# Reading matmul operands backwards and weaving the two words of each weight, in four forms

## The chip, the cores and the metric

The kernel runs on one core of a Trainium2 chip. The metric is the device time of one execution in microseconds; three runs of the kernel before gave 804.3 to 804.74 us with a median of 804.55 us. The core has a matrix engine (TensorE; in the views PE for its matmuls and PEld for its weight loads), a vector engine (VectorE, DVE), a scalar engine (ScalarE, ACT), GpSimd (POOL), and DMA queues that SyncE (SP) issues here.

## The reference

Everything is in 32-bit floating point. A retention layer (attention with a decay in place of a softmax) is followed by two multilayer perceptrons (MLPs) over 2304 tokens of 512 values:

```python
scores = scale * np.matmul(q, k.transpose(0, 1, 3, 2))
ret = scores * Dmat[None, :, :, :]                 # decay by distance, causal
x = np.matmul(ret, v)                              # (4, 8, 576, 64) -> (2304, 512)
...
h = np.maximum(x @ w_in, 0.0)                      # first MLP, 512 -> 2048
x = h * h @ w_out                                  # 2048 -> 512
...
h = x @ w_in2                                      # second MLP, 512 -> 2048
g = h * np.clip(h + 3.0, 0.0, 6.0) / 6.0
out = g @ w_out2                                   # 2048 -> 512
```

## The kernel before, in words

A product of two 32-bit numbers is made from three matmuls in a shorter format (float32r). Each operand is split into a high word (a cast) and a low word (the operand minus its high word), and a product is high times high, plus low times high, plus high times low. Every tile that a matmul reads therefore has a dimension of 2: index 0 is the high word, index 1 the low one.

**First MLP.** Tokens go in five blocks of 512, 384, 512, 384 and 512 (BLOCKS); a block's tokens are the columns that move through TensorE. The hidden dimension goes in 16 tiles of 128, numbered f. For each f there are two weight tiles, w_f_0 (for w_in) and w_f_1 (for w_out), each with 128 partitions, two words and 512 values. They are loaded and split once, in the first block, and stay for all five. The split is cast_w on ScalarE (the high word, L167) and low_w on GpSimd or VectorE (the low word, L174). h_part (L623) makes one hidden tile h with 12 matmuls: three products of words by four slices of 128 input values. ScalarE and VectorE turn h into the two words of its squared positive part, the tile g. a_part (L660) adds that tile's share to the four accumulators acc with 12 matmuls. The main loop emits h_part for the next f ahead of a_part for this one, so TensorE's order is h of f+1, acc of f, h of f+2, acc of f+1, and so on. In between stand the small matmuls of the retention layer for later tokens (L408 to L496) and, on the other engines, the preparation of the second MLP's weights.

**Second MLP.** It runs in three superblocks s of 768 tokens, each as seven products of half size in place of eight (Strassen's scheme in Winograd's form). In each superblock first come 336 matmuls of 384 columns (L1183, out to the PSUM banks z, weights from the tiles ring, columns from the tiles xop), and then 504 matmuls of 256 columns (L1238, weights from the tiles spl, columns from ring).

Where tiles lie in SBUF is set by the order of allocation and by three tiles that nothing uses: `align` (80 values) moves what lies on the right side, and `shift0` and `shift1` move the tiles spl by 64 bytes:

```python
    SHIFT, FIRST_SHIFT = 64 // 4, 192 // 4
    p1a.tile([P, SHIFT], F32, tag="shift0", name="shift0")
```

With these, the operands of L623, L660 and L1183 all begin at the same place modulo 512 bytes, and the weights of L1238 begin 64 bytes (modulo 128) away from its columns.

The program's order is written out by hand (manual_schedule); each engine runs its instructions in that order.

Of the kernel before, what the change touches and what calls it, by code (L numbers as in the profile page):

```python
# [12 lines left out]
F32R = mybir.dt.float32r  # L13
# [73 lines left out]
def retention_moe_kernel(ctx: ExitStack, tc, qk, kv, w1, w2, cst, out):  # L87
# [30 lines left out]
    ctx.enter_context(tc.manual_schedule())  # L118


    raws = {}
    wts = {}
    narrowed = [0]
# [38 lines left out]
    def cast_w(ph, f, halves=(0, 1)):  # L162

        for i in halves:
            t = wts[ph, f, i]
            w = (wlo if f < NJ else whi).tile([P, 2, DM], F32R, tag=f"w{f}_{i}", name=f"w_{ph}_{f}_{i}")
            nc.scalar.activation(w[:, 0, :], t, AF.Copy)  # L167
            wts[ph, f, i] = w, t

# [441 lines left out]
    def h_part(ph, blk, f, between=lambda: None):  # L611
        nb = BLOCKS[blk][0]
        w = wts[ph, f, 0]
        x = xs[ph, blk]
        hp = ps_h.tile([P, 512], F32, tag="h", name=f"h_{ph}_{blk}_{f}")
        def order(last):
            return [(c, wi, xi) for wi, xi in ((0, 0), last[::-1], last) for c in range(NC)]

        parts = 2 if ph == blk == f == 0 else 1
        for i in range(parts):  # L620
            ts = slice(i * nb // parts, (i + 1) * nb // parts)
            for k, (c, wi, xi) in enumerate(order((1, 0) if blk == 0 and i == 0 else (0, 1))):
                nc.tensor.matmul(  # L623
                    hp[:, ts],
                    w[:, wi, c * P : (c + 1) * P],
                    x[:, xi, c, ts],
                    start=k == 0,
                    stop=k == 3 * NC - 1,
                )
        r = tmpp.tile([P, 512], F32, tag="tmp", name=f"r_{ph}_{blk}_{f}")  # L630
        r = r[:, :nb]
        nc.scalar.activation(r, hp[:, :nb], AF.Relu)  # L632
        between()
        nc.vector.tensor_tensor(r, r, hp[:, :nb], ALU.mult)  # L634
        g = gpool.tile([P, 2, 512], F32R, tag="g", name=f"g_{ph}_{blk}_{f}")
        nc.scalar.activation(g[:, 0, :nb], r, AF.Copy)  # L636
        gts[ph, blk, f] = g, r
# [7 lines left out]
    def a_part(ph, blk, f):  # L645
        nb = BLOCKS[blk][0]
        w = wts[ph, f, 1]
        g = gts.pop((ph, blk, f))
        if f == 0:
            two = [  # L650
                ps_acc.tile([P, 2, 512], F32, tag="acc", name=f"acc_{ph}_{blk}_{d}")
                for d in range(2)
            ]
            accs[ph, blk] = [two[d // 2][:, d % 2, :] for d in range(NC)]
        acc = accs[ph, blk]
        last = f == NF - 1

        def mm(d, wi, gi, first, stop):
            wt = w[:, wi, d * P : (d + 1) * P]
            nc.tensor.matmul(acc[d][:, :nb], wt, g[:, gi, :nb], start=first, stop=stop)  # L660

        if last:
            for d in range(NC):
                mm(d, 0, 0, False, False)
                mm(d, 1, 0, False, False)
                mm(d, 0, 1, False, True)
        else:
            for d in range(NC):
                mm(d, 0, 0, f == 0, False)
                mm(d, 1, 0, False, False)  # L670
            for d in range(NC):
                mm(d, 0, 1, False, False)
# [488 lines left out]
    for s in range(SUPERS):  # L1161
        t_a = now + NJ * 7 * t_in

        for m, (q, k) in enumerate((q, k) for q in ORDER for k in range(NJ)):
            free = t_a + (m - NSPL + 1 + 1.6 * ((s, q) == FINAL and k >= NSPL)) * t_out / NJ
            if m < NSPL:
                free = max(free, now + (k + 1) * 7 * t_in + 1.0)
            at(free + 0.1, a_cast, s, q, k)
            at(free + 0.7, a_low, s, q, k)
        for j in range(NJ):  # L1170
            e = j % 2
            bank = {q: z[k][:, :HALF] for q, k in H_BANK[e].items()}
            s1, u2 = held[2 * e][:, 0, :], held[2 * e][:, 1, :]
            u3 = held[1][:, e, :]
            c22, c21, c12 = s1, u3, u2
            for i, q in enumerate(ORDER):
                run(now)
                w = wring[s, 0, j, i // 2][:, i % 2]
                x = x_ops[q]
                for k, (u, wi, xi) in enumerate(  # L1180
                    [(u, wi, xi) for wi, xi in ((0, 0), (1, 0), (0, 1)) for u in range(2)]
                ):
                    nc.tensor.matmul(  # L1183
                        bank[q],
                        w[:, wi, u * P : (u + 1) * P],
                        x[:, u, xi, :],
                        start=k == 0 and q not in (2, 4, 3),
                        stop=k == 5,
                        skip_group_check=q in (2, 4, 3),
                    )  # L1190
                now += t_in
                if i % 2 or i == 6:
                    ring_done(now + 0.1)
                if q == 1:
                    at(now, act, s1, bank[1], AF.Copy)
                elif q == 6:
                    at(now, tt, u2, bank[6], s1, ALU.add)
                elif q == 7:
                    at(now, tt, u3, bank[7], u2, ALU.add)
                elif q == 5:  # L1200
                    at(now, tt, c22, bank[5], u3, ALU.add)
                    at(now + 0.8, relu3, 4, j, c22)
                    at(now + 1.3, gate, 4, j, c22)
                elif q == 2:
                    at(now, relu3, 1, j, bank[1])
                    at(now + 0.75, gate, 1, j, bank[1])
                elif q == 4:
                    at(now, tt, c21, bank[4], u2, ALU.add)
                    at(now + 0.8, relu3, 2, j, c21)
                    at(now + 1.3, gate, 2, j, c21)  # L1210
                else:
                    at(now, tt, c12, bank[3], u2, ALU.add)
                    at(now + 0.8, relu3, 7, j, c12)
                    at(now + 1.3, gate, 7, j, c12)
                    at(now + 2.0, pool_op, 5, 7, 4, ALU.add, j)
                    at(now + 2.1, pool_op, 7, 1, 7, ALU.subtract, j)
                    at(now + 2.2, pool_op, 6, 5, 1, ALU.subtract, j)
                    at(now + 2.3, pool_op, 3, 2, 6, ALU.subtract, j)
        if s + 1 < SUPERS:
            for u, st in enumerate(x_stages(s + 1)):  # L1220
                for k, part in enumerate(st):
                    at(now + 1.0 + 25.0 * u * (k > 0) + 3.0 * k + 4.0 * (k > 0), do, part)
        s1, u3, u2 = [h.rearrange("p a b -> p (a b)") for h in held]
        for i, q in enumerate(ORDER):
            work = [(k, (0, 1, 2)) for k in range(NJ)]
            if (s, q) == FINAL:

                work = [(k, (0, 1)) for k in range(LAG)]
                for k in range(NJ):
                    work += [(k, (2,))] + [(k + LAG, (0, 1))] * (k + LAG < NJ)  # L1230
            to = {2: (0, 0, None), 5: (1, 1, u3), 4: (1, 0, u2), 3: (0, 1, u2)}
            for k, parts in work:
                run(now)
                w, sp = wring[s, 1, q, k // 2], splits[s, q, k]
                for n in parts:
                    o = z[A_BANKS[q][n // 2]][:, HALFD * (n % 2) : HALFD * (n % 2 + 1)]
                    for m, (g, wi) in enumerate(((0, 0), (0, 1), (1, 0))):
                        nc.tensor.matmul(  # L1238
                            o,
                            sp[:, g, P * n : P * (n + 1)],  # L1240
                            w[:, k % 2, wi, :],
                            start=k == 0 and m == 0 and n % 2 == 0 and q not in (2, 4, 3),
                            stop=k == NJ - 1 and m == 2 and n > 0,
                            skip_group_check=q in (2, 4, 3),
                        )
                now += t_out / NJ / NTT * len(parts)
                if k % 2 and 2 in parts:
                    ring_done(now + 0.1)
                if q in to and k == NJ - 1:
                    pieces = [i for i in range(2) if PIECES[i][0] in parts]  # L1250
                    at(now, emit, now, s, q, *to[q], pieces)
            if q not in to:
                at(now, merge, q, *{1: (s1, None), 6: (u2, s1), 7: (u3, u2)}[q])
# [39 lines left out]
```

## Time and profile before

| what | before |
|---|---|
| device time, median of 3 runs | 804.55 us (804.3 to 804.74) |
| span of the profiled execution, first to last instruction | 802.6 us |
| TensorE matmuls busy, instructions | 796.4 us (99%), 6380 |
| TensorE weight loads busy, instructions | 741.0 us (92%), 6380 |
| VectorE, ScalarE, GpSimd busy | 591.9, 397.5, 167.7 us |
| TensorE's granted clock, mean | 1.000 |

The profiled execution has no device time of its own on record: its span is 802.6 us, and the median of the runs is 1.95 us more. A matmul's duration in the profile reaches from its start to a modelled end, and matmuls overlap, so the rate of a row of them is read from the distance of their starts: the pieces of the chain of waits give that, as a time and a count of matmuls. The number in front of a piece is its start in us from the start of the span.

### The profile page before, as it was taken

To read this page: it belongs to the slowest core of one execution; us is meant where nothing else is said; L and a number is where in the kernel's file an instruction comes from. 1 tells how busy PE (TensorE), PEld (TensorE's weight loads), DVE (VectorE), ACT (ScalarE), POOL (GpSimd) and SP (SyncE) were. 2 spreads that over 40 slices of the span, in tenths; PEclk is the share of its full clock that TensorE was granted. 3 is DMA by queue.
4 is the path that set the end of the run, shared out by engine and by line. 5 is a ranking of instruction groups with operands and counts; after the bars stand their busy time and mean duration, and the time that the engine had idled before them with its cause. 6 is when DMAs were issued, how large, how long until landed. Compare 5 with 4: busy or idle time off the path is not lost.

```text
span 802.6 us, 16522 instructions
## 1 busy us (share of the span) xinstructions
PE 796.4 (99%) x6380; PEld 741.0 (92%) x6380; DVE 591.9 (74%) x1086; ACT 397.5 (50%) x738; POOL 167.7 (21%) x161
## 2 busy tenths in 40 slices
PE   8999999999999999999999999999999999999998
PEld 8788889999888899998888899999999999999998
DVE  5989987887755577776557867997577987677864
ACT  2797745444443444444435533666234655244553
POOL 4412130211011011100000065500255500256300
PEclk9999999999999999999999999999999999999999
DMA  9957626777756487856448797888887979877884
GB/s 331 352 189 248 223 93 203 225 214 222 222 157 184 124 260 212 234 158 184 145 130 269 242 303 256 306 307 291 274 264 242 353 261 302 279 240 266 272 274 139
DMA packets 148494, 189.64 MB, mean 236 GB/s; under 512 B 22592, under 2 KB 102080, under 8 KB 148416
## 3 DMA queue, kind: packets, MB, share of 16 engines
q1 hardware_dynamic: 148416, 188.59, 73.5%
q8 instruction: 50, 0.82, 0.4%
q14 instruction: 28, 0.23, 0.1%
HBM read 149.76 MB, written 38.80 MB: 235 GB/s over the span
## 4 chain that ended last, share of the span: by engine, by line
PE 95%; DMA 3%; DVE 1%; SPq 0%; ACT 0%; issue 0%; DVEq 0%
PE acc L660 24%; PE h L623 24%; PE z L1183 22%; PE z L1238 21%; PE at L496 2%; DMA raw<-w_dram 1%; DMA v<-kv_dram 1%; DMA kv<-kv_dram 1%; PE alone L496 0%; PE sc L408 0%; PE o L459 0%; PE sc L419 0%; DVE wt L158 0%; DVE wt L159 0%; PE o L469 0%; ACT w L167 0%
## 5 line engine op out<-in xcount | busy, mean ns | idle before, releaser
L660 PE MATMUL acc<-g,w 128*128 128x512 f32 (+1 forms) x960 | 213.3, 370 | 0.4 <-ACT g L636 0.4
L623 PE MATMUL h<-x,w 128*128 128x512 f32 (+2 forms) x972 | 210.6, 365 | 0.2 <-ACT w L167 0.2
L660 PEld LDWEIGHTS acc<-g,w 128*128 128x128 f32 x960 | 173.6, 188 | 25.2 <-ACT g L636 0.8
L623 PEld LDWEIGHTS h<-x,w 128*128 128x128 f32 x972 | 175.7, 188 | 22.8 <-ACT w L167 0.6
L1183 PE MATMUL z<-xop,ring 128*128 128x384 f32 x1008 | 175.2, 334 | 0.0
L1183 PEld LDWEIGHTS z<-xop,ring 128*128 128x128 f32 x1008 | 174.7, 188 | 0.1
L1238 PE MATMUL z<-ring,spl 128*128 128x256 f32 x1512 | 172.2, 276 | 0.0
L1238 PEld LDWEIGHTS z<-ring,spl 128*128 128x128 f32 x1512 | 172.1, 188 | 0.0
L1099 POOL TENSOR_TENSOR aop<-aop,aop 128x384 f32<-128x384 f32 x96 | 106.2, 1116 | 296.2 <-DVE aop L1096 292.4
L1121 DVE TENSOR_TENSOR spl<-aop,spl 128x384 fp32r<-128x384 f32 x168 | 100.5, 617 | 30.7 <-ACT spl L1117 29.4
L1117 ACT ACTIVATE spl<-aop 128x384 fp32r<-128x384 f32 x168 | 86.3, 523 | 54.7 <-PE z L1238 49.8
L632 ACT ACTIVATE r<-h 128x512 f32<-128x512 f32 (+1 forms) x80 | 44.3, 553 | 110.7 <-PE h L623 110.4
L1093 ACT ACTIVATE aop<-held,small 128x384 f32<-128x384 f32 x72 | 44.4, 617 | 108.4 <-DVE held L1059 107.8
L634 DVE TENSOR_TENSOR r<-r,h 128x512 f32<-128x512 f32 (+1 forms) x80 | 50.5, 632 | 53.9 <-ACT r L632 53.5
L1059 DVE TENSOR_TENSOR held<-z,held 128x384 f32<-128x384 f32 x120 | 66.4, 553 | 28.9 <-PE z L1183 26.7
L636 ACT ACTIVATE g<-r 128x512 fp32r<-128x512 f32 (+1 forms) x80 | 47.2, 590 | 65.8 <-DVE r L634 65.8
L642 DVE TENSOR_TENSOR g<-r,g 128x512 fp32r<-128x512 f32 (+1 forms) x80 | 54.7, 684 | 21.0 <-ACT g L636 18.5
L1096 DVE SCALAR_TENSOR_TENSOR aop<-aop,held 128x384 f32<-128x384 f32 x72 | 49.9, 692 | 17.7 <-ACT aop L1093 16.1
L393 POOL TENSOR_TENSOR qs<-qs,con 128x512 f32<-128x512 f32 x11 | 14.7, 1340 | 136.3 <-DMA qs<-qk_dram 123.9
L750 ACT ACTIVATE uhi<-seven 128x896 fp32r<-128x896 f32 x32 | 30.6, 955 | 23.7 <-DVE seven L740 14.0
L755 DVE TENSOR_TENSOR seven<-seven,uhi 128x896 fp32r<-128x896 f32 x32 | 34.9, 1089 | 7.3 <-ACT uhi L750 7.0
L174 POOL TENSOR_TENSOR w<-wt,w 128x512 fp32r<-128x512 f32 x17 | 22.7, 1336 | 62.9 <-ACT w L167 60.2
(111 smaller groups left out, 609.8 us busy)
## 6 DMA issues: line engine op xcount, KB each, us to landing
ring<-w_out_hl SPq DMA_DIRECT2D x84, 512.0 KB, 4.9
ring<-w_in_hl SPq DMA_DIRECT2D x72, 512.0 KB, 4.7
raw<-w_dram SPq DMA_DIRECT2D x32, 512.0 KB, 7.1
uraw<-w_dram SPq DMA_DIRECT2D x64, 256.0 KB, 3.2
q<-qk_dram SPq DMA_DIRECT2D x17, 512.0 KB, 5.3
w_in_hl<-uhi SPq DMA_DIRECT2D x16, 448.0 KB, 3.4
w_in_hl<-seven SPq DMA_DIRECT2D x16, 448.0 KB, 4.8
w_out_hl<-uhi SPq DMA_DIRECT2D x16, 448.0 KB, 3.2
```

Of the source, the lines that this page charges most:

```text
L623: nc.tensor.matmul(hp[:, ts], w[:, wi, c * P : (c + 1) * P], x[:, xi, c, ts], start=k == 0, stop=k == 3 * NC - 1,)
L634: nc.vector.tensor_tensor(r, r, hp[:, :nb], ALU.mult)
L636: nc.scalar.activation(g[:, 0, :nb], r, AF.Copy)
L642: nc.vector.tensor_tensor(g[:, 1, :nb], r, g[:, 0, :nb].bitcast(F32), ALU.subtract)
L660: nc.tensor.matmul(acc[d][:, :nb], wt, g[:, gi, :nb], start=first, stop=stop)
L1059: fn(*a)
L1096: stt(f32(q, j), f32(q, j), 6.0, h, ALU.min, ALU.mult)
L1099: nc.gpsimd.tensor_tensor(f32(o, j), f32(a, j), f32(b, j), op)
L1117: act(t[:, 0, :], f32(q, k), AF.Copy)
L1121: tt(t[:, 1, :], f32(q, k), t[:, 0, :].bitcast(F32), ALU.subtract)
L1183: nc.tensor.matmul(bank[q], w[:, wi, u * P : (u + 1) * P], x[:, u, xi, :], start=k == 0 and q not in (2, 4, 3), stop=k == 5, skip_group_ch ...
L1238: nc.tensor.matmul(o, sp[:, g, P * n : P * (n + 1)], w[:, k % 2, wi, :], start=k == 0 and m == 0 and n % 2 == 0 and q not in (2, 4, 3), st ...
```

## The change

No instruction is added, removed or moved. On each engine the same instructions stand in the same order before and after, and they wait for the same semaphores, except that one VectorE instruction (a gate of the middle superblock, L1096) now also waits for TensorE, as the ScalarE instruction before it on the same data does already. All tiles keep their places. What changes is the order in which some operands are read or written.

In the first MLP it goes by the tile number f:

- f % 4 = 0: as before.
- f % 4 = 1: backwards. The matmuls of h_part read the columns of x from the last to the first, so h, its square and g hold the tokens in reverse; the matmuls of a_part read g from the last column to the first, so the accumulators get the tokens in their usual order.
- f % 4 = 2: woven. High and low word of a weight lie side by side, so the 128 columns of a weight load, and what the cast and the subtraction write, lie 8 bytes apart in place of 4.
- f % 4 = 3: both.

In the middle superblock of the second MLP (s = 1) every matmul reads its columns backwards and writes its output backwards, so the results lie as before.

```diff
@@ -118,6 +118,15 @@
     ctx.enter_context(tc.manual_schedule())
 
 
+    def woven(f):
+        return f % 4 >= 2
+
+    def backwards(f):
+        return f % 2 == 1
+
+    def turned(ap, yes):
+        return ap[:, ::-1] if yes else ap
+
     raws = {}
     wts = {}
     narrowed = [0]
@@ -163,7 +172,11 @@
 
         for i in halves:
             t = wts[ph, f, i]
-            w = (wlo if f < NJ else whi).tile([P, 2, DM], F32R, tag=f"w{f}_{i}", name=f"w_{ph}_{f}_{i}")
+            p, name = wlo if f < NJ else whi, f"w_{ph}_{f}_{i}"
+            if woven(f):
+                w = p.tile([P, DM, 2], F32R, tag=f"w{f}_{i}", name=name).rearrange("p n t -> p t n")
+            else:
+                w = p.tile([P, 2, DM], F32R, tag=f"w{f}_{i}", name=name)
             nc.scalar.activation(w[:, 0, :], t, AF.Copy)
             wts[ph, f, i] = w, t
 
@@ -623,7 +636,7 @@
                 nc.tensor.matmul(
                     hp[:, ts],
                     w[:, wi, c * P : (c + 1) * P],
-                    x[:, xi, c, ts],
+                    turned(x[:, xi, c, ts], backwards(f)),
                     start=k == 0,
                     stop=k == 3 * NC - 1,
                 )
@@ -657,7 +670,8 @@
 
         def mm(d, wi, gi, first, stop):
             wt = w[:, wi, d * P : (d + 1) * P]
-            nc.tensor.matmul(acc[d][:, :nb], wt, g[:, gi, :nb], start=first, stop=stop)
+            gt = turned(g[:, gi, :nb], backwards(f))
+            nc.tensor.matmul(acc[d][:, :nb], wt, gt, start=first, stop=stop)
 
         if last:
             for d in range(NC):
@@ -1181,9 +1195,9 @@
                     [(u, wi, xi) for wi, xi in ((0, 0), (1, 0), (0, 1)) for u in range(2)]
                 ):
                     nc.tensor.matmul(
-                        bank[q],
+                        turned(bank[q], s == 1),
                         w[:, wi, u * P : (u + 1) * P],
-                        x[:, u, xi, :],
+                        turned(x[:, u, xi, :], s == 1),
                         start=k == 0 and q not in (2, 4, 3),
                         stop=k == 5,
                         skip_group_check=q in (2, 4, 3),
@@ -1236,9 +1250,9 @@
                     o = z[A_BANKS[q][n // 2]][:, HALFD * (n % 2) : HALFD * (n % 2 + 1)]
                     for m, (g, wi) in enumerate(((0, 0), (0, 1), (1, 0))):
                         nc.tensor.matmul(
-                            o,
+                            turned(o, s == 1),
                             sp[:, g, P * n : P * (n + 1)],
-                            w[:, k % 2, wi, :],
+                            turned(w[:, k % 2, wi, :], s == 1),
                             start=k == 0 and m == 0 and n % 2 == 0 and q not in (2, 4, 3),
                             stop=k == NJ - 1 and m == 2 and n > 0,
                             skip_group_check=q in (2, 4, 3),
```

## Rows read from the trace of the kernel before

**Rows 1.** The page: busy time, and 40 slices in tenths.

```profile
PE 796.4 (99%) x6380; PEld 741.0 (92%) x6380; DVE 591.9 (74%) x1086; ACT 397.5 (50%) x738; POOL 167.7 (21%) x161
...
PE   8999999999999999999999999999999999999998
...
PEclk9999999999999999999999999999999999999999
```

**Rows 2.** The page: chain that ended last, shares by line.

```profile
PE acc L660 24%; PE h L623 24%; PE z L1183 22%; PE z L1238 21%; PE at L496 2%; DMA raw<-w_dram 1%; DMA v<-kv_dram 1%; DMA kv<-kv_dram 1%; PE alone L496 0%; PE sc L408 0%; PE o L459 0%; PE sc L419 0%; DVE wt L158 0%; DVE wt L159 0%; PE o L469 0%; ACT w L167 0%
```

**Rows 3.** All waits of TensorE: total us, times, longest us.

```profile
PE unread L851 <- POOL early L845: 1.0, 1, 1.0
PE o L292 <- POOL v L267: 0.5, 1, 0.5
PE o L292 <- POOL kv L267: 0.4, 1, 0.4
PE acc L660 <- ACT g L636: 0.4, 1, 0.4
PE o L302 <- POOL states L348: 0.2, 1, 0.2
PE h L623 <- ACT w L167: 0.2, 1, 0.2
```

**Rows 4.** Chain of waits, first MLP: start us, us, what.

```profile
45.13 2.72 PE h L623 x12
...
303.54 2.08 PE h L623 x12
305.62 2.08 PE acc L660 x12
```

**Rows 5.** Chain of waits, second MLP.

```profile
452.82 58.27 PE z L1183 x336
511.09 57.18 PE z L1238 x504
568.27 58.24 PE z L1183 x336
626.51 57.32 PE z L1238 x504
```

**Rows 6.** Weight loads by form: busy us, mean ns.

```profile
L660 PEld LDWEIGHTS acc<-g,w 128*128 128x128 f32 x960 | 173.6, 188 | 25.2 <-ACT g L636 0.8 <-DVE g L642 0.6 <-POOL w L174 0.3
...
L408 PEld LDWEIGHTS sc<-q 64*64 64x64 f32 x128 | 2.2, 134 | 1.4 <-issue 1.1 <-DVE g L642 0.4
```

**Rows 7.** Timeline, TensorE, from 24.0 us to 25.3 and to 25.4.

```profile
23.75 1.72 PE L623 MATMUL h<-x,w 128*128 128x256 f32 x13
23.75 1.84 PE L623 MATMUL h<-x,w 128*128 128x256 f32 x14
```

**Rows 8.** Matmuls of a_part by form: busy us, mean ns.

```profile
L660 PE MATMUL acc<-g,w 128*128 128x512 f32 x576 | 140.4, 392 | 0.4 <-ACT g L636 0.4
...
L660 PE MATMUL acc<-g,w 128*128 128x384 f32 x384 | 72.9, 337 | 0.0
```

**Rows 9.** Weight preparation by form: stride 8 bytes (L140, L158), contiguous (L167).

```profile
L140 ACT ACTIVATE raw<-raw 128x512 f32<-128x512 f32 x32 | 21.3, 666 | 1.0 <-DMA raw<-w_dram 1.0
L167 ACT ACTIVATE w<-wt 128x512 fp32r<-128x512 f32 x32 | 19.9, 623 | 4.0 <-DVE wt L159 3.9
L158 DVE TENSOR_SCALAR wt<-raw 128x512 int32<-128x512 int32 x32 | 16.3, 508 | 0.6 <-ACT raw L140 0.6
```

**Rows 10.** Chain of waits where the width changes between groups (113 to 123 us).

```profile
112.88 2.72 PE h L623 x12
115.60 2.72 PE acc L660 x12
118.32 2.10 PE h L623 x12
120.42 2.76 PE acc L660 x12
```

**Rows 11.** Timeline of the first block: subtractions, and matmuls that read them.

```profile
61.45 1.42 POOL L174 TENSOR_TENSOR w<-wt,w 128x512 fp32r<-128x512 f32 x1 [4.42 <-ACT w L167]
...
62.60 2.88 PE L623 MATMUL h<-x,w 128*128 128x512 f32 x12
...
64.78 0.68 DVE L174 TENSOR_TENSOR w<-wt,w 128x512 fp32r<-128x512 f32 x1
...
66.50 3.02 PE L660 MATMUL acc<-g,w 128*128 128x512 f32 x12
```

## Prediction, made before the changed kernel ran

> **What bounds the kernel now.** I read the page's first two parts first: TensorE is busy 796.4 us of a span of 802.6 us, and in 38 of the 40 slices for at least nine tenths of the time, with the granted clock at full speed throughout [rows 1]. That alone doesn't say that its matmuls run at their best, because the busy time of pipelined matmuls overlaps. The chain of waits is the next view: 24% + 24% + 22% + 21% of it are the four matmul lines [rows 2]. The list of what TensorE waited for is the third: six waits, once each, 2.7 us in all [rows 3]. So the time is, apart from the start, the number of matmuls times the spacing from one to the next, and a change that alters the spacing moves the end by just that much.
>
> The spacing is read from the chain's long pieces, where nothing but one line runs. Twelve 512-column matmuls of the first MLP take 2.72 us, so 226.7 ns each; twelve of 384 columns 2.08 us, so 173.3 ns [rows 4]. In the second MLP 336 matmuls of 384 columns take 58.27 us (173.4 ns) and 504 of 256 columns 57.18 us (113.5 ns) [rows 5]. At a granted clock of 1.00, which is 2.4 GHz, a column a cycle would be 213.3, 160.0 and 106.7 ns. So every matmul carries an extra: 13.3 ns at 512 columns, 13.3 at 384, 13.4 in L1183, 6.8 in L1238. It doesn't grow with the columns. Each matmul has one weight load beside it [rows 6], so I take the extra to be the price of that load's reads beside the matmul's own.
>
> Two rows say that the extra depends on where the two operands lie. The only other 256-column matmuls are the 24 of the first tile: 13 of them from 23.75 us on take 1.72 us and 14 take 1.84, so one more is 0.12 us, or 120 ns, an extra of 13.3 [rows 7]. L1238 has the same shape and an extra of only half of that; what differs is that its weights (spl) stand 64 bytes off (SHIFT). The rate of each stream is read from durations: a weight load of 128 columns takes 188 ns and one of 64 takes 134 to 135 [rows 6], so 0.84 ns a weight column; a matmul of 512 columns takes 392 ns and one of 384 takes 337 [rows 8], so 0.43 ns a moving column. Weights thus advance through memory at half the speed of the moving columns.
>
> **The change part by part.** Nothing is added or taken away: the same instructions stand in the same order on each engine, with one wait more on VectorE, behind an ACT operation that waits for the same matmuls already, so it costs nothing. What changes is the access pattern of 2280 matmuls, 16 casts and 16 subtractions.
>
> Counts: each f of the first MLP has 24 matmuls a block, over five blocks. Each of the four forms has 4 of the 16 tiles, so 480 matmuls: 288 of 512 columns and 192 of 384 (the first tile's halves are of the unchanged form). The middle superblock has 336 (L1183) and 504 (L1238).
>
> *Woven weights (f % 4 = 2 and 3, 960 matmuls).* A weight column now steps 8 bytes in 0.84 ns, which is the 4 bytes in 0.43 ns of the moving stream. The two streams stop sweeping past each other. No row shows such a pair. Bounds: the extra goes (960 x 13.3 = 12.8 us gained), or it doubles because the load touches twice the span of bytes (12.8 us lost). I take the nearest better relation that rows show, 6.7 ns: 960 x 6.65 = 6.4 us gained.
>
> *Whether a stride of 8 bytes slows a load.* The nearest rows are on other engines: ScalarE's conversion in place at that stride takes 666 ns for 512 columns against 623 for the contiguous cast, and VectorE's read at that stride 508 [rows 9]. A reader of one column a tick is thus hardly slowed; I take nothing.
>
> *Backwards alone (f % 4 = 1, 480 matmuls).* It turns the direction in which the streams pass each other and leaves their speeds. Bounds: 480 x 13.3 = 6.4 us gained, or as much lost. I take nothing, between the two.
>
> *Middle superblock.* Bounds: L1183's extra gone, 336 x 13.4 = 4.5 us, and L1238's, 504 x 6.8 = 3.4; or L1238 loses what its 64 bytes gave, 504 x 6.5 = 3.3 us lost, and L1183 doubles, 4.5 lost. I take nothing.
>
> *Changing form every twelve matmuls.* Tiles of h run one ahead of those of acc, so from one group of twelve to the next the form now always changes. Where the width changes between groups today, twelve 512-column matmuls take 2.76 us instead of 2.72, and twelve of 384 take 2.10 instead of 2.08 [rows 10]: the spacing needs some matmuls to settle. There are 160 groups. Bounds: nothing, and 160 x 0.04 = 6.4 us lost. The width changes the spacing by 53 ns, a form only by some 7, so I take a quarter, 0.01 us: 1.6 us lost.
>
> *Casts and subtractions to woven tiles.* All lie in block 0. By ScalarE's two rows the stride adds 7%: 0.04 us a cast, 0.05 a VectorE subtraction, 0.09 a GpSimd one. Cover: GpSimd's subtraction of 61.45 us ends at 62.87, and the matmuls from 62.60 us read its result last, in their ninth, at 64.4 us: 1.5 us to spare. VectorE's of 64.78 ends at 65.46, for matmuls from 66.50 us: 1.0 us to spare [rows 11]. So nothing. If the cover were gone, eight of each at the full surplus would cost 1.1 us.
>
> Sum: - 6.4 + 1.6 = - 4.8 us. The profiled span is 802.6 us and the median of the three runs 804.55, 1.95 us more around it, which the change doesn't touch. So 804.55 - 4.8 = **799.7 us**.
>
> **A rule that speaks against a gain.** The Trainium skill, page "TensorE: Matmul & The Clock Gate", section "Part 2: What happens when you issue a matmul", says that weight loads have a read port of their own and take no read bandwidth from the running matmul. By that the extra isn't a collision and no form changes it: 804.5 us. The trace half disagrees: 120 against 113.5 ns at one shape [rows 5, 7]. It is the second rival.
>
> **The rivals.**
>
> *More gain (15%).* The reversal helps as much as the weave: 1440 x 6.65 = 9.6 us and L1183 336 x 6.7 = 2.2, less 1.6 of settling: 794.3 us. With every extra gone it would be 777. For it: one relation in two already shows half. Against: nothing in the trace reads backwards.
>
> *No change (12%).* The extra belongs to the load itself, and L1238 has less because at 256 columns load and matmul are equally long (128 x 0.84 = 108 ns). All forms keep 13.3 and nothing needs to settle: 804.5 us.
>
> *Slower by settling (18%).* At every seam of two forms the spacing is unsettled and costs the full 0.04 us of the width's seams, 160 times, while the weave gains nothing: 804.55 + 6.4 = 811 us. It decides as soon as a seam costs more than 0.04 us against the full gain, or 0.01 without one. For it: the spacings at the width's seams; against: they follow a far larger change.
>
> *Woven loads at half rate (9%).* If a column of weights takes 1.68 ns at the stride, a load takes 215 ns. 512-column matmuls hide it (215 + 6.8 is under 226.7), 384-column ones don't: 2 x 192 x (221.8 - 173.3) = 18.6 us: 823 us. Against: ScalarE's 7%.
>
> *Backwards reads or writes at half rate (6%).* 960 matmuls of the first MLP (576 x 213 + 384 x 160 ns = 184 us), 336 x 160 + 504 x 107 ns = 108 in the middle: 1096 us, or less if only the middle's writes suffer. The Trainium skill, page "Advanced Engine Details and Errata", section "Memory Cachelines", says that any access pattern to PSUM that isn't contiguous slows matmuls much, but asks only that two consecutive elements lie together. By its first sentence the middle superblock's outputs, written backwards, would slow; by its second they wouldn't, and no run here shows it yet.
>
> **How the numbers follow.** The forecast has 40%, its own range 794 to 803 (its bounds on backwards and middle, half used). The 80% range is 788 to 816: it leaves out the two half-rate cases (15%) and some 5% at the ends. A measurement of this kernel tells 0.2%, 1.6 us, from no change. Faster: 37 of the forecast's 40 and the first rival, 52%. Same: the no-change rival and the forecast's other 3, 15%. Slower: the rest, 33%.
>
> **What would show it.** In the chain, twelve-matmul groups of woven f at about 2.64 us for 512 columns and 2.00 for 384, and those of f % 4 = 0 and 1 at 2.72 and 2.08; the middle superblock at 58.2 and 57.3 us like the other two; no new wait of TensorE. I am wrong if woven groups stay at 2.72 or grow, if groups of the unchanged form f % 4 = 0 grow (settling), or if the middle superblock moves.

## The result, and the profile after

The changed kernel takes 815.26 us (median of 4 runs, 814.96 to 815.5) against 804.53 us before (4 runs): a ratio of 1.0134 with a 95% interval of 1.0121 to 1.0146. It is 10.7 us slower. The time lies inside the range, on the other side of no change from the forecast. The profiled span grew by 10.6 us, from 802.6 to 813.2 us.

The page's busy times and granted clock, which answer to [rows 1], say only that TensorE is still the bound at full clock:

```profile
PE 808.0 (99%) x6380; PEld 751.8 (92%) x6380; DVE 592.6 (73%) x1086; ACT 400.1 (49%) x738; POOL 167.2 (21%) x161
...
PEclk9999999999999999999999999999999999999999
```

All waits of TensorE after (us in total, times, longest), which answer to [rows 3]:

```profile
PE unread L865 <- POOL early L859: 1.0, 1, 1.0
PE acc L674 <- ACT g L649: 0.4, 1, 0.4
PE o L305 <- POOL kv L280: 0.2, 1, 0.2
PE h L636 <- ACT w L180: 0.2, 1, 0.2
```

These are four of the six from before, 1.8 us in place of 2.7. TensorE waits less and ends later, so all of the loss is in the spacing of matmuls. (Line numbers have moved: h_part's matmul is L636, a_part's L674, those of the second MLP L1197 and L1252.)

The chain of waits in the third block, which has 512 columns; it answers to [rows 4]. The columns are start, time, what:

```profile
202.02 2.80 PE h L636 x12
204.82 2.74 PE acc L674 x12
207.56 2.80 PE h L636 x12
...
215.39 2.80 PE h L636 x12
218.19 2.80 PE acc L674 x12
220.99 2.73 PE h L636 x12
223.71 2.81 PE acc L674 x12
```

Read with the order of tiles, these are h of f = 1 (backwards), acc of 0 (as before), h of 2 (woven), h of 3 (both), acc of 2 (woven), h of 4 (as before), acc of 3 (both). Every changed form takes 2.80 to 2.81 us, so 233.3 ns a matmul in place of 226.7, and the unchanged form 2.73 to 2.74.

The same view in the fourth block, 384 columns: h of f = 1 (backwards), acc of 0 (as before), h of 2 (woven), then h of 3 (both) and acc of 2 (woven).

```profile
297.16 2.13 PE h L636 x12
299.30 2.09 PE acc L674 x12
301.38 2.08 PE h L636 x12
...
307.82 2.13 PE h L636 x12
309.95 2.08 PE acc L674 x12
```

Here the woven form costs nothing more (2.08), and the two that read backwards take 2.13, which is 177.5 ns in place of 173.3.

The second MLP's pieces of the chain, which answer to [rows 5]:

```profile
459.78 58.25 PE z L1197 x336
518.03 57.18 PE z L1252 x504
575.21 59.73 PE z L1197 x336
634.93 59.49 PE z L1252 x504
694.42 58.24 PE z L1197 x336
```

It starts 7.0 us later than before, and its middle superblock alone is longer: 59.73 for 58.24 us (177.8 ns a matmul for 173.3) and 59.49 for 57.32 (118.0 for 113.7).

**Where the 10.6 us are.** Each form has 24 groups of twelve matmuls at 512 columns and 16 at 384. Backwards: 24 x 0.08 + 16 x 0.05 = 2.7 us. Woven: 24 x 0.08 = 1.9. Both: 2.7. The middle superblock: 1.49 + 2.17 = 3.7. That is 11.0 us; 0.9 us of waits are gone. What remains, some 0.5 us, fits the groups of the unchanged form, which take 0.01 to 0.03 us longer than before; but with pieces read to 0.01 us it is no more than rounding could make of so many groups.

### The profile page after: what moved, and what is told of

It reads as the page before. It is cut to its first block, busy times and chain, and to the rows that moved or that the text cites. A ratio compares the mean times of both kernels' runs of the same rounds, so it can differ in the third digit from the quotient of the medians.

```text
span 813.2 us, 16522 instructions
## 1 busy us (share of the span) xinstructions
PE 808.0 (99%) x6380; PEld 751.8 (92%) x6380; DVE 592.6 (73%) x1086; ACT 400.1 (49%) x738; POOL 167.2 (21%) x161
## 4 chain that ended last, share of the span: by engine, by line
PE 97%; DVE 2%; ACT 1%; issue 0%; POOL 0%; DVEq 0%; POOLq 0%
PE acc L674 25%; PE h L636 24%; PE z L1197 22%; PE z L1252 21%; PE at L509 2%; PE unread L865 1%; PE sc L288 1%; DVE wt L167 0%; PE alone L509 0%; DVE wt L168 0%; PE sc L421 0%; PE o L305 0%; ACT w L180 0%; PE o L472 0%; PE sc L432 0%
## 5 line engine op out<-in xcount | busy, mean ns | idle before, releaser
L674 PE MATMUL acc<-g,w 128*128 128x512 f32 (+1 forms) x960 | 216.8, 375 | 0.4 <-ACT g L649 0.4
L636 PE MATMUL h<-x,w 128*128 128x512 f32 (+2 forms) x972 | 214.5, 370 | 0.2 <-ACT w L180 0.2
L636 PEld LDWEIGHTS h<-x,w 128*128 128x128 f32 x972 | 178.9, 192 | 23.5 <-ACT w L180 0.6
L674 PEld LDWEIGHTS acc<-g,w 128*128 128x128 f32 x960 | 176.7, 192 | 25.3 <-ACT g L649 0.8
L1197 PE MATMUL z<-xop,ring 128*128 128x384 f32 x1008 | 176.7, 336 | 0.0
L1197 PEld LDWEIGHTS z<-xop,ring 128*128 128x128 f32 x1008 | 176.2, 188 | 0.1
L1252 PE MATMUL z<-ring,spl 128*128 128x256 f32 x1512 | 174.4, 278 | 0.0
L1252 PEld LDWEIGHTS z<-ring,spl 128*128 128x128 f32 x1512 | 174.3, 188 | 0.0
```

The lines of the kernel that those rows point to most:

```text
L636: nc.tensor.matmul(hp[:, ts], w[:, wi, c * P : (c + 1) * P], turned(x[:, xi, c, ts], backwards(f)), start=k == 0, stop=k == 3 * NC - 1,)
L674: nc.tensor.matmul(acc[d][:, :nb], wt, gt, start=first, stop=stop)
L1197: nc.tensor.matmul(turned(bank[q], s == 1), w[:, wi, u * P : (u + 1) * P], turned(x[:, u, xi, :], s == 1), start=k == 0 and q not in (2, 4 ...
L1252: nc.tensor.matmul(turned(o, s == 1), sp[:, g, P * n : P * (n + 1)], turned(w[:, k % 2, wi, :], s == 1), start=k == 0 and m == 0 and n % 2 ...
```

## The experiments

Three theories, with the letters that the expectations use. **A:** the extra of a matmul (its spacing less one column a cycle) depends on the order in which its moving reads visit places, relative to the places that the next weight load reads; the kernel before stands at a cheap relation, and every changed form leaves it. **B:** reading backwards, or weights 8 bytes apart, has a price of its own, at any place. **C:** the price lies at the seams, since the form changes with each group of twelve.

**A sweep of places (s1_places).** A kernel with nothing but rows of 24 equal matmuls, each row with its own form, width and distance between the places of weights and columns, while the other engines stand idle:

```python
def plain(off, i, m):
    s = off // 4 + 128 * (i % 4)
    return w[:, s : s + m]
def woven(off, i):
    s = off // 4 + 256 * (i % 4) + (i // 4) % 2
    return w[:, s : s + 256 : 2]
...
for i in range(24): nc.tensor.matmul(z[:128, :512], plain(64, i, 128), cols(512, i, False), start=True, stop=True)
```

> Leaves out the whole computation: only rows of 24 equal matmuls, each with a weight load, one row for each pair of form (forwards, backwards, woven, both) and distance in bytes between weights and columns, at 512, 384 and 256 columns. Theory A (the reads of the next weight load and of the running matmul collide by place): the spacing depends on the distance within a form; forwards at 512 columns 226.7 ns at distance 0, less at others; at 256 columns 120 ns at 0 and 113.3 at 64; at distance 0, 233.3 ns backwards and woven, as in the changed kernel. Theory B (a reversed or stepped read has a price of its own): backwards 233.3 and woven 233.3 ns at every distance. Theory C (what costs is the change of form every twelve matmuls): 226.7 ns at 512 columns in all forms, once a row has settled. Weights of 64 columns: by A the extra of 13.3 ns halves, by a fixed price of a load it stays.

The chain, 24 matmuls a piece. The granted clock is 1.00 over these rows. In order, at 512 columns: forwards at distances of 0, 64, 128 and 256 bytes (L48, L52, L54, L57), backwards at 0 and 64 (L61, L65), woven at 0 and 64 (L74, L76), both at 0 (L82). Then 384 columns: forwards at 0 (L90) and backwards at 0 (L103). Then 256 columns: forwards at 0, 64 and 320 (L126, L130, L136), backwards at 64 (L143).

```profile
26.74 5.44 PE z L48 x24
...
48.82 5.59 PE z L52 x24
...
60.02 5.57 PE z L54 x24
...
76.70 5.46 PE z L57 x24
...
98.84 5.60 PE z L61 x24
...
121.25 5.60 PE z L65 x24
...
171.65 5.60 PE z L74 x24
...
182.81 5.52 PE z L76 x24
...
216.16 5.60 PE z L82 x24
...
260.97 4.16 PE z L90 x24
...
315.40 4.26 PE z L103 x24
...
412.50 2.87 PE z L126 x24
...
423.88 2.73 PE z L130 x24
...
440.90 2.83 PE z L136 x24
...
460.82 2.83 PE z L143 x24
```

The rows give back every spacing of the two kernels, with no seams and no other engine at work: 226.7 ns (5.44 / 24) forwards at distance 0, 233.3 (5.60) for each changed form, 173.3 and 177.5 at 384 columns, 113.7 and 117.9 at 256 and 64 bytes. So C falls. Forwards, the distance alone moves a matmul between 226.7 and 233.3 ns, and at 256 bytes the spacing is back, which is A. At 512 columns the rows at 320, 384 and 448 bytes repeat those at 64, 128 and 192 to 0.01 us; at 384 and 256 columns they do not all: 64 and 320 bytes give 4.16 and 4.24 us, and 2.73 and 2.83.

Backwards at 512 columns gave 5.60 at every distance from 0 to 448 bytes, which is what B expects as well. The woven rows go against B: at 512 columns they move with the distance between 5.52 and 5.60, and at 384 columns and 0 bytes they cost no more than forwards (4.16, L110).

Two things that I had expected of A did not come. At 512 columns other distances cost more than 0, not less. And weights of 64 columns did not halve the extra there: their row at 0 bytes takes 5.52 us (L168), which is 230.0 ns, 3.3 ns more than with weights of 128.

In all 42 rows of 512 columns none is under 5.44, and in the 36 of 384 none under 4.16; at 256 columns the cheapest, 2.73, is what L1238 has. Of the forms and distances tried, the kernel before has the cheapest of each width, but for the 24 matmuls of its first tile (120 ns [rows 7]).

**One form for all tiles (e1_back_all, e2_woven_all).** Every f but the first tile in one form, the middle superblock as before. Each differs from the changed kernel by:

```diff
-        return f % 4 >= 2          # woven
+        return False               # e1; e2: return f > 0
-        return f % 2 == 1          # backwards
+        return f > 0               # e1; e2: return False
-                        turned(bank[q], s == 1),
+                        turned(bank[q], False),
```

and the three other s == 1 likewise.

> All tiles of the first MLP but f = 0 backwards, nothing woven, middle superblock as before. In the changed kernel's chain twelve backwards matmuls take 2.80 us instead of 2.72 at 512 columns and 2.13 instead of 2.08 at 384. Theories A and B: 30 groups a block x (3 x 0.08 + 2 x 0.05) = 10.2 us more than before, 814.7 us. Theory C (seams): with one form nearly everywhere no seams are left, 804.5 us.

> All tiles of the first MLP but f = 0 woven, nothing backwards. Twelve woven matmuls take 2.80 us at 512 columns and 2.08 at 384 in the changed kernel. Theories A and B: 30 x 3 x 0.08 = 7.2 us more, 811.7 us, all of it in the blocks of 512 tokens. Theory C: 804.5 us.

All backwards: 813.78 us, ratio 1.0116 (1.0101 to 1.0131). All woven: 811.43 us, ratio 1.0084 (1.0069 to 1.0099). With the seams all but gone the loss is there for each changed group, so C falls in the kernel too. In the chains a group of 512 columns takes 2.80 us in both, and one of 384 takes 2.13 in e1_back_all (the first pair of lines) and its old 2.08 in e2_woven_all (the second).

```profile
203.01 2.80 PE h L636 x12
...
309.21 2.13 PE h L636 x12
```

```profile
202.41 2.80 PE h L636 x12
...
308.47 2.08 PE h L636 x12
```

Fifteen of 16 tiles make 90 groups of 512 and 60 of 384: 90 x 0.08 + 60 x 0.05 = 10.2 us for e1 (measured 9.5), and 90 x 0.08 = 7.2 us for e2 (measured 7.1).

**The middle superblock alone (e3_middle_only).** woven and backwards return False, and the four s == 1 stay.

> Only the middle superblock backwards, the first MLP as before. By the changed kernel's chain: L1183's group there 59.73 us instead of 58.24, L1238's 59.49 instead of 57.32, together 3.7 us more: 808.2 us by theories A and B. By theory C there is one seam only: 804.5 us.

808.93 us, ratio 1.0056 (1.004 to 1.0073): 4.6 us more by the medians, 3.7 us by the two pieces of the chain below, which are the changed kernel's; the profiled execution, at 808.19 us, was the shortest of its four.

```profile
568.41 59.73 PE z L1197 x336
628.13 59.49 PE z L1252 x504
```

An estimate from the three runs: eight of 16 tiles read backwards in the changed kernel, four of them woven too at no more than that in the chain, so 8/15 of e1's 9.5 us is 5.1; four are woven alone, so 4/15 of e2's 7.1 is 1.9; with 3.7 to 4.6 for the middle superblock this makes 10.7 to 11.6 us, against 10.7 measured. One more thing can be read here: these matmuls also write their output backwards, and cost 177.8 ns (59.73 / 336); those of L103 in the sweep read backwards and write forwards, for 177.5. At 256 columns it is 118.0 against 117.9 (L143). Writing backwards thus cost nothing here. The Trainium skill, page "Advanced Engine Details and Errata", section "Memory Cachelines", says that any access to PSUM that isn't contiguous slows matmuls much; of its two sentences only the second, that pairs of elements should lie together, agrees with this.

**Distance alone, in the kernel before (e4_align_less, e5_shift_128).** Nothing is read backwards or woven; an unused tile is made smaller or larger, so that operands stand elsewhere to each other. The first moves the tiles on the right side by 64 bytes, the second five in six of the weights of L1238 from 64 to 128 bytes off their columns.

```diff
-    pool(ctx, "align", 1, side="right").tile([P, 80], F32, tag="align", name="align")
+    pool(ctx, "align", 1, side="right").tile([P, 64], F32, tag="align", name="align")   # e4
-    SHIFT, FIRST_SHIFT = 64 // 4, 192 // 4
+    SHIFT, FIRST_SHIFT = 128 // 4, 192 // 4                                             # e5
```

> The kernel before with the unused tile align of 64 values in place of 80: nothing is read backwards and nothing is woven, the right side's tiles lie 64 bytes lower. By theory A and the rows of s1_places (512 columns forwards at distance 64: 233.3 instead of 226.7 ns; 384 columns: no difference): the 569 matmuls of 512 columns whose operands lie on different sides cost 6.6 ns more each, 3.8 us, and some 425 of L1238 4 to 6.7 ns more, 1 to 2 us: 809 to 810 us. By theory B (only the direction or the step has a price): 804.3 us.

> The kernel before with SHIFT of 128 bytes in place of 64: the weights of L1238 stand 128 bytes off its columns, forwards and contiguous as before. By theory A and s1_places (256 columns forwards at distance 128: 118.3 instead of 113.3 ns) the 1258 matmuls with moved weights cost 5.0 ns more, 6.3 us: 810.6 us. By theory B: 804.3 us.

809.56 us, ratio 1.0063 (1.0048 to 1.0078), as A expects, and 811.87 us, ratio 1.0094 (1.0077 to 1.0111), 1.3 us more than A expects. The chain of e5_shift_128 shows the same line that the change hit, at 118.6 ns a matmul in place of 113.5, and L1183 as before (58.27):

```profile
510.78 59.77 PE z L1238 x504
```

A place can thus cost as much as a backward read. The three pieces of L1238 are 7.6 us longer together, which is 6.0 ns for each matmul with moved weights, in place of the 5.0 expected from the sweep; why wasn't found.

**Is it the direction, or the order of places? (s2_blocks, e6_blocks_64, e7_blocks_16).** Columns are read in blocks, the last block first, but inside a block forwards. By B, a block order has a step back only where a block ends, and should cost nothing or little at any size; by A it costs something as long as a block is short against the 256 bytes after which the sweep repeats at 512 columns.

```python
        return t.rearrange("p (a b) -> p a b", b=int(mode[1:]))[:, ::-1]
```

The mode "b16", say, stands for blocks of 16 columns, 64 bytes.

> Leaves out the whole computation: rows of 24 equal matmuls as in the run s1_places, with further conditions. Columns in blocks of 4, 16, 32, 64, 128 or 256, the blocks from last to first and each block forwards, 512 columns at distance 0: if the price of going backwards comes from the order of the places that the reads visit (theory A), large blocks keep the forward spacing of 226.7 ns over most of their length and small ones reach 233.3; if it comes from the reversed single read (theory B), all blocks stay at 226.7, and only blocks of one column would cost. Columns 8 bytes apart: by A another spacing than 226.7, by B 233.3 or more. Both operands moved by the same 16 to 128 bytes: by A 226.7 wherever the distance is kept at 0. Widths between 256 and 512: an extra of 32 cycles or more for all at distance 0 (13.3 ns), if no width escapes it.

The chain, 24 matmuls a piece, all but L72 at distance 0; the granted clock is 1.00. 512 columns forwards, with weights and columns both moved by 16 bytes (L59); in blocks of 4 (L64), 16 (L67), 32 (L70; L72 at a distance of 128 bytes) and 64 (L73); 384 columns in blocks of 4 (L82), 16 (L83) and 64 (L84); 512 columns that lie 8 bytes apart (L85), and 256 such (L89).

```profile
71.64 5.54 PE z L59 x24
...
99.07 5.60 PE z L64 x24
...
115.87 5.60 PE z L67 x24
...
132.75 5.58 PE z L70 x24
...
143.83 5.47 PE z L72 x24
149.30 5.44 PE z L73 x24
...
199.14 4.26 PE z L82 x24
203.41 4.24 PE z L83 x24
207.65 4.16 PE z L84 x24
211.81 10.88 PE z L85 x24
...
255.33 5.44 PE z L89 x24
```

At distance 0 a block order of up to 32 columns, which is 128 bytes, costs nearly what the full reversal does; from 64 columns, 256 bytes, it costs nothing. Blocks of 32 with the weights 128 bytes further come down to 5.47 (L72): the same order is dear at one distance and nearly free at another, as A has it.

Two expectations did not come out. With weights and columns moved by the same 32 to 128 bytes the row stays near the 5.45 of distance 0 (5.47), but moved by 16 bytes it takes 5.54 (L59), so the distance is not all that counts. And not every width at distance 0 has an extra of 13.3 ns or more: at 288 columns it is 11.7 (L127: 3.16 us for 24).

In the kernel the block orders went the way of their rows. Nothing is woven in either run; e6 reads in blocks of 64 in every f but the first and in the middle superblock, and e7 in blocks of 16 in every f but the first (middle as before):

```diff
-        return ap[:, ::-1] if yes else ap
+        return ap.rearrange("p (a b) -> p a b", b=64)[:, ::-1] if yes else ap   # e6; e7: b=16
```

> The changed kernel with nothing woven and with reversal in blocks: blocks of 64 columns (256 bytes) are taken from last to first, each block forwards, in all tiles of the first MLP but f = 0 and in the middle superblock, its outputs too. The rows of s2_blocks give 226.7 ns for 512 columns in such blocks and 173.3 for 384, as forwards. If only the order of places inside 256 bytes matters: nothing lost, 804.4 us. If any order but the plain one costs what backwards did: 10.2 us for the first MLP (e1 measured 9.5) and 3.7 for the middle, 817 us.

> As e6_blocks_64, but blocks of 16 columns (64 bytes), in the first MLP's tiles f > 0 alone. By s2_blocks such rows take 233.3 ns at 512 columns and 176.7 at 384, though 15 of 16 single reads go forwards: 30 groups x 12 x (3 x 6.6 + 2 x 3.4 ns) = 9.6 us lost, 814 us. If what costs is a single read that steps back, only one in 16 does, and under 1 us is lost: 805 us.

Blocks of 64: 804.45 us (11 runs) against 804.47, ratio 0.9999 (0.999 to 1.0008). Blocks of 16: 813.05 us, ratio 1.0104 (1.009 to 1.0118). The chain of e6_blocks_64 in its middle superblock, and one group of 512 columns of e7_blocks_16:

```profile
568.31 58.25 PE z L1197 x336
626.55 57.32 PE z L1252 x504
```

```profile
208.27 2.80 PE h L636 x12
```

B falls for reading backwards too: a group that steps back at one column in 16 costs the full 2.80 us in e7, and e6, which does visit its blocks in reverse, costs nothing. Of the three theories A is left. That it is the next weight load, and not the matmul's own, whose places count was not tested.

No version beats the kernel before. None of the forms and distances tried has at 512 or 384 columns an extra below the 13.3 ns that it has now; e6, the best of the changed ones, equals it.

## Why the prediction was wrong

**The bound, right.** The time is the number of matmuls times their spacing. No wait came in, and the pieces of the chain account for the whole loss.

**The extra depends on the places of the two operands, right.** The sweep moves it from 13.3 to 20.0 ns at 512 columns and from 12.9 to 7.1 at 256 (2.87 and 2.73 us for 24) by the distance alone. The rival that held the extra to be the load's own is refuted by this: a load that only reads from another place delays the row by 6.6 ns a matmul. The Trainium skill, page "TensorE: Matmul & The Clock Gate", section "Part 2: What happens when you issue a matmul", has the rule that loads take no read bandwidth from the running matmul; the rows of this sweep don't agree with it.

**"I take the extra to be the price of that load's reads", shown for a part only.** The part that moves with the place is; a floor stays. At 512 columns, weights of 64 columns, whose loads are shorter (134 against 188 ns [rows 6]), have an extra of 16.7 ns and not less (L168 of the first sweep); at 256 columns and distance 0 they do help, with 2.73 us for 24 (L149 of the second sweep) in place of 2.87.

**The woven term, wrong: this is the step that failed.** "I take the nearest better relation that rows show, 6.7 ns: 960 x 6.65 = 6.4 us gained." The 6.7 ns came from a row of 256 columns and was carried to 512 and 384, where no distance or form in the sweeps comes under 13.3. The weave moved the 512-column matmuls to 20.0 ns: 48 groups at 0.08 us are 3.8 us lost, and the form "both" at 384 columns loses 0.8 more. The argument behind it, that streams of equal speed stop sweeping past each other, said that the relation changes, not that the new one is better. At 512 columns the old one was the best of all that were tried.

**Backwards, mis-sized.** I took nothing, between bounds of 6.4 us either way; it lost 24 x 0.08 + 16 x 0.05 = 2.7 us, by the same mechanism.

**The middle superblock, mis-sized.** Nothing was taken; it lost 3.7 us. The bound for L1238, "504 x 6.5 = 3.3 us lost", had the right mechanism: it gave back two thirds of what its 64 bytes had brought.

**Settling, mis-sized.** The unchanged form among changed ones takes 2.73 to 2.74 us for 2.72, and 2.09 to 2.11 for 2.08. The balance of the whole leaves some 0.5 us where I had put 1.6. The rival "slower by settling" named the right side with the wrong cause, and it is the one rival on the slow side that the range takes in: that the measured time lies inside is luck.

**Loads and casts at the stride, right.** Woven groups of 384 columns stay at 2.08 us, so the loads don't run at half rate. ScalarE's casts, half of them now at the stride, went from a mean of 623 [rows 9] to 650 ns, and TensorE's wait for them is the 0.2 us of before. By form, with busy us and mean ns:

```profile
L180 ACT ACTIVATE w<-wt 128x512 fp32r<-128x512 f32 x32 | 20.8, 650 | 3.4 <-DVE wt L168 3.4
```

**Open.** What in the memory makes the relation of places matter wasn't found. The runs show a repeat after 256 bytes at 512 columns but not at every distance at 384 and 256, a row that moves when weights and columns are moved together by 16 bytes, and at distance 0 a difference between orders in blocks of 128 bytes and of 256; they don't show why the extra stops at 13.3 ns at 512 and 384 columns.

## What to carry to other kernels

When TensorE is busy throughout, divide a long piece of the chain by its count of matmuls. A part of what lies above one column a cycle depends on where weights and columns lie and on the order in which they are read, and here up to 6.6 ns of it over 1440 matmuls and a superblock made 1.3% of the time. Before an operand is reordered or moved, a single short kernel of rows of equal matmuls tells what each relation costs, at each width apart; a good row at one width says nothing of another. If columns must be read in another order, blocks that keep 256 bytes together cost nothing here.

## What the runs showed of the hardware that was not expected

Columns 8 bytes apart double a matmul: 453.3 ns for 512 columns (L85: 10.88 / 24) against 226.7, and 226.7 for 256 (L89). Weights 8 bytes apart cost at most 6.7 ns against contiguous ones at the same distance (L74 against L48 of the first sweep). The Trainium skill, page "SBUF — State Buffer", section "Specifications (TRN2)", asks for two hits in a 16-byte line for full bandwidth; columns 8 bytes apart have two, so by that rule nothing would be lost, and for TensorE's moving operand the measurement decides against it.

The order of places matters at distances of a few bytes: with the columns forwards, moving the weights alone by 4 to 12 bytes at 512 columns already costs 3 to 5 ns a matmul in the second sweep (5.52 to 5.57 us for 24), while moving weights and columns together by 32 to 128 bytes leaves the row at 5.47. Sixteen bytes behave the other way: the weights alone moved by them take 5.45 (L49 of the first sweep), weights and columns together 5.54.
